# Summing the logits of a sliding-window attention by one reduction, and storing outputs by half tiles

## The chip, the core and the metric

The kernel runs on one core of a Trainium2 chip. The core has TensorE (PE, the matrix multiplier, which reads SBUF and accumulates in PSUM), VectorE (DVE), ScalarE (ACT), GpSimd (POOL) and SyncE (SP, which here only issues DMA transfers). Each engine runs its own instructions in the order in which they were written into the program; semaphores make it wait for others. SBUF is the working memory of 128 partitions, PSUM holds the accumulators in eight banks, of which a 128x512 f32 tile fills one. The metric is the device time of one execution in microseconds (us).

## What is computed

Four layers in a row on a 2048x1024 activation: attention (A), a gated unit (B), A, B, each behind a layer norm and with a residual added. The attention has 32 heads of 32 features and looks at 8 positions, two apart, at or before the query's own:

```
qkv = (x @ wqkv).reshape(B, S, 3, H, Dh)           # H = 32, Dh = 32
idx = pos[:, None] - arange(8)[None, :] * 2        # masked where idx < 0
logits = einsum("bhsd,bhswd->bhsw", q, kg) * Dh**-0.5
attn = softmax(where(mask, logits, -1e9))
o = einsum("bhsw,bhswd->bhsd", attn, vg);  return o.reshape(B, S, D) @ wo
# B: gate = x @ W_gate; up = x @ W_up; (relu(gate) * up) @ W_down, with F = 3584
```

So one logit is a sum over the 32 features of q times a k that lies w*2 positions back. The change is about this sum, and about how the last layer's result goes to memory.

## The kernel before, in words

The 2048 rows are cut into four blocks of 512 (`NB` = 4), each of four tiles of 128 rows (`TPB` = 4). PE does, for each block, the q, k and v projections (`plan_proj`, L364), the output projection (`plan_wo`, L642), gate and up (`plan_gu`, L672) and down (`plan_down`, L718). Every one of these is eight-matmul (or, in down, longer) accumulations into a PSUM tile from one pool of eight (tag `acc`), which is handed round in order. Weights come as slabs of 1 MB through a ring of five buffers (`RING`), loaded by SP (L196) as soon as PE has finished with the slab that had the buffer.

The attention core is not on PE, but on DVE, in "head-major" form: q, k and v go to DRAM and come back with (row tile, head) on the partitions and (feature, position) along the free dimension (L498). For each w of 0 to 7, DVE multiplies q with the shifted k into `pr`, 32 features x 128 positions in bf16, feature outermost (`mul`, L512). Then it sums over the features: `add3` (L522) adds blocks of 8 features three times into an f32 tile `l` of 8x128, and `fold` (L529, L530) halves `l` three times, the last add writing row w of the logits `L`. After eight w comes the softmax in two parts (`soft_a`, L537 to L542, then an exponential on ACT, L545, then `soft_b`, L550 to L555) and eight groups of a times v (`pv_mul`, L563, `pv_add`, L571 to L573), whose results POOL sends to DRAM (L574) and SP fetches back as `oT` (L582) for the output projection. Block 0 of the first layer gets its logits in another way (`first_logits`, on PE); the other seven blocks, three of the first attention layer and four of the second, go through `mul`, `add3` and `fold`: 56 times in all.

DVE also empties PSUM: it multiplies up with the ReLU of gate into `hT` (L687; ACT makes the ReLU `r`, L679, with three buffers), and adds the output projection (L649) and down (L726) to the residual x. ACT copies q, k and v out of PSUM (L373) and does the layer-norm passes (L219, L220, L244).

The order of everything is planned by hand. `Plan` lets each step be booked at a time; PE's order follows from the count of matmuls alone. DVE's attention work is a chain of items `(ready, duration, function, after)`, walked in order by `_place_dve`; the emptying of PSUM and the layer-norm scalars are "fixed" items with due times, and are put in between two chain items as soon as their due time has come. A chain item is not interrupted. The durations in the plan are written out: 2.25 us for `mul`, 1.27 for each of the three adds, 1.5 for `fold`. All other queues (ACT's exponential, SP's loads of q, k, v, POOL's stores) get their place from the times that this walk gives. On the chip nothing is re-ordered.

In the last layer `plan_down` stores the result. For each half (512 columns) of down, and each of the four row tiles, `add` puts the sum into x; for blocks 0 to 2, the store of the full 128x1024 tile (L732, SP) is issued after the second half; for the last block each half is stored by itself (L730, SP or ACT).

Of the kernel before, what the change touches and what calls it, by code (L numbers as in the profile page):

```python
# [10 lines left out]
F32 = mybir.dt.float32  # L11
ALU = mybir.AluOpType
ACT = mybir.ActivationFunctionType

P = 128
D = 1024
H = 32
DH = 32
W = 8
# [4 lines left out]
TPB = BLK // P  # L24
EPS = 1e-5
NEG = -1.0e9
SLAB = 512
# [12 lines left out]
def _ap(t, off, dims):  # L40
    return bass.AP(tensor=t.tensor, offset=t.offset + off, ap=[list(t.ap[0])] + [list(d) for d in dims])
# [78 lines left out]
def kernel(  # L120
# [11 lines left out]
    nc = tc.nc  # L132
# [9 lines left out]
    out_dram = out.flatten_outer_dims()  # L142
# [14 lines left out]
    at_pool = ctx.enter_context(tc.tile_pool(name="attn", bufs=1))  # L157
# [32 lines left out]
    def slab(src_ap, name, start=-10.0):  # L190
        shp = list(src_ap.shape)

        def load():
            t = wring.tile([P, 8, SLAB], BF16, tag="slab", name=name)
            s["t"] = t[:, 0:shp[1], 0:shp[2]]
            nc.sync.dma_start(s["t"], src_ap)  # L196

        s = plan.slab(load, start)
        return s

    plan = Plan(RING)
# [288 lines left out]
    def plan_attn(L, b, ends, st, tm):  # L490
# [16 lines left out]
        def mul(w):  # L507
            def f():
                if w == 0:
                    st["L"] = at_pool.tile([P, W, P], F32, tag="L", name=f"L_{L}_{b}")  # L510
                pr = at_pool.tile([P, DH, P], BF16, tag="pr", name="pr", bufs=2)
                nc.vector.tensor_tensor(pr[:], st["q"][:], _ap(st["k"], HALO - DIL * w, [[HALO + P, DH], [1, P]]),  # L512
                                        op=ALU.mult)
                st["pr"] = pr
            return f

        def add3(i):
            def f():
                if i == 0:
                    st["l"] = at_pool.tile([P, 8, P], F32, tag="l1", name="l1")  # L520
                l, pr = st["l"], st["pr"]
                nc.vector.tensor_tensor(l[:], pr[:, 0:8] if i == 0 else l[:], pr[:, 8 * i + 8:8 * i + 16], op=ALU.add)  # L522
            return f

        def fold(w):
            def f():
                l = st["l"]
                for n in (4, 2):
                    nc.vector.tensor_tensor(l[:, 0:n], l[:, 0:n], l[:, n:2 * n], op=ALU.add)  # L529
                nc.vector.tensor_tensor(st["L"][:, w, :], l[:, 0], l[:, 1], op=ALU.add)  # L530
            return f

        def soft_a():
# [69 lines left out]
        now = lambda: 0.0  # L603
        first = L == 0 and b == 0
        for w in range(0, 0 if first else W):
            plan.chain.append((qk_ready if w == 0 else now, 2.25, mul(w), None))
            for i in range(3):
                plan.chain.append((now, 1.27, add3(i), None))
            plan.chain.append((now, 1.5, fold(w), (lambda t: tm.__setitem__("logits", t)) if w == W - 1 else None))

        def after_a(t):
            plan.at(t + 0.2, expo)
# [88 lines left out]
    def plan_down(L, b, st, last):  # L701
        nsl = (FC + 7) // 8
        accs = {}
        end = last and b == NB - 1

        def cols(half, t):

            n = 2 if end and (half, t) == (1, TPB - 1) else 1
            return [(half * SLAB + i * SLAB // n, SLAB // n) for i in range(n)]

        def mms(half, s8, w, nfc, t):
            def f():
                for c0, n in cols(half, t):
                    if s8 == 0:
                        accs[(t, c0)] = psum.tile([P, n], F32, tag="acc", name="dacc")
                    for jl in range(nfc):
                        j = 8 * s8 + jl
                        nc.tensor.matmul(accs[(t, c0)][:], lhsT=st["hT"][:, j, t * P:(t + 1) * P],  # L718
                                         rhs=w["t"][:, jl, c0 - half * SLAB:c0 - half * SLAB + n],
                                         start=(j == 0), stop=(j == FC - 1))  # L720
            return f

        def add(half, t, c0, n):
            def f():
                xt = x_tiles[b * TPB + t]
                nc.vector.tensor_tensor(xt[:, c0:c0 + n], accs.pop((t, c0))[:], xt[:, c0:c0 + n], op=ALU.add)  # L726
                r0 = (b * TPB + t) * P
                if end:
                    eng = nc.scalar if t == 1 or (t == TPB - 1 and c0 == SLAB) else nc.sync
                    eng.dma_start(out_dram[r0:r0 + P, c0:c0 + n], xt[:, c0:c0 + n])  # L730
                elif last and half == 1:
                    nc.sync.dma_start(out_dram[r0:r0 + P, :], xt[:])  # L732
            return f

        for half in range(2):
            for s8 in range(nsl):
                nfc = min(8, FC - 8 * s8)
                w = slab(wd_v[:, 8 * s8:8 * s8 + nfc, half * SLAB:(half + 1) * SLAB], f"wd_{L}_{b}_{half}_{s8}")
                for t in range(TPB):
                    e = plan.on_pe(nfc, mms(half, s8, w, nfc, t), [w])  # L740
                    if s8 == nsl - 1:
                        pieces = cols(half, t)
                        for i, (c0, n) in enumerate(pieces):
                            plan.on_dve(e + T_EV - 0.4 * (len(pieces) - 1 - i), 0.7, add(half, t, c0, n))
# [9 lines left out]
    def proj(L, b):  # L754
        st, tm = {}, {}
        if L == 0 and b == 0:
            hooks, later_hooks[:] = (lambda h: (h[0], [h[1]]))(first_logits(st, tm))
        else:
            hooks = later_hooks.pop() if later_hooks else {}
        attn[(L, b)] = plan_attn(L, b, plan_proj(L, b, hooks), st, tm)  # L760
# [95 lines left out]
```

## Time and profile before

| | |
|---|---|
| median of 3 runs | 1622.98 us (1622.66 to 1623.08) |
| profiled execution, its own time | 1622.84 us |
| its span in the trace | 1621.1 us |
| PE busy | 1611.6 us (99%) |
| DVE busy | 1014.6 us (63%) |
| ACT busy, POOL busy | 458.1 us, 109.3 us |
| TensorE clock granted | 1.0 throughout |
| DMA moved | 314.83 MB, mean 194 GB/s |
| time of one w on DVE (a `mul`, three adds, a fold), no other work between | 7.49 us (136.30 to 143.79) |

The span runs from the first to the last thing that the profiler saw of the program; the execution's own time has 1.7 us more around it. Busy time of PE is the time in which a matmul is under way. DVE's share of 63% is a mean: until 1255 us, where the last block's attention ends, it is some 90% busy in most stretches, and after that 10 to 20%. Rows of the profile give a line, an engine, the operation, out<-in, the shapes, the count, the busy time, the mean duration of one in ns, and the idle time before them with what ended it.

### The profile page before, as it was taken

How to read it: one execution, taken by the hardware profiler on the slowest of the kernel's cores; microseconds unless marked ns; L12 is line 12 of the kernel's file. 1: busy time of each engine (PE TensorE's matmuls, PEld its weight loads, DVE VectorE, ACT ScalarE, POOL GpSimd, SP SyncE). 2: the span in 40 equal slices, each digit the busy share in tenths (PEclk: the TensorE clock that was granted, in tenths of full speed). 3: DMA queues.
4: the chain of work that ended last, by engine and by line, in shares of the span. 5: the costliest groups of instructions: out<-in, count | busy, mean ns of one | idle time of the engine just before them, and what ended most of it. 6: DMA issues, size and time to landing. Idle time of an engine off the chain costs nothing.

```text
span 1621.1 us, 19223 instructions
## 1 busy us (share of the span) xinstructions
PE 1611.6 (99%) x7641; PEld 740.6 (46%) x7690; DVE 1014.6 (63%) x1256; ACT 458.1 (28%) x735; POOL 109.3 (7%) x174
## 2 busy tenths in 40 slices
PE   9999999999999999999999999999999999999999
PEld 5444444444444444444444444444444444444444
DVE  4576999989989069960699616986989212211211
ACT  6564421304131241312413251133011311221110
POOL 3221000001001100011000110000000000000000
PEclk9999999999999999999999999999999999999999
DMA  8799798597866988669876699599846655565452
GB/s 240 163 199 192 191 218 210 167 217 193 219 173 211 223 206 208 188 200 234 202 198 196 213 223 226 158 279 240 216 154 194 172 182 162 176 173 165 156 167 67
DMA packets 444203, 314.83 MB, mean 194 GB/s; under 512 B 195504, under 2 KB 438608, under 8 KB 444112
## 3 DMA queue, kind: packets, MB, share of 16 engines
q1 hardware_dynamic: 414944, 281.39, 66.7%
q10 hardware_dynamic: 24368, 23.40, 4.7%
q0 software_dynamic: 4800, 8.80, 1.8%
q8 instruction: 60, 0.98, 0.3%
q14 instruction: 31, 0.25, 0.1%
HBM read 261.77 MB, written 36.05 MB: 184 GB/s over the span
## 4 chain that ended last, share of the span: by engine, by line
PE 99%; DMA 0%; DVE 0%; issue 0%; SPq 0%; POOL 0%; DVEq 0%; POOLq 0%
PE acc_g L672 24%; PE acc_u L672 24%; PE dacc L718 24%; PE acc_v L364 7%; PE acc_k L364 7%; PE acc_wo L642 7%; PE acc_q L364 7%; DMA x<-in_A_x_dram 0%; PE L L464 0%; DVE bst L294 0%; POOL rstd L318 0%; DVE xn_all L323 0%; DVE x L726 0%; SPq L785 0%; DVE xnT L331 0%
## 5 line engine op out<-in xcount | busy, mean ns | idle before, releaser
L672 PE MATMUL acc_u<-xnT,wu 128*128 128x512 bf16 x1792 | 423.3, 379 | 0.0
L672 PE MATMUL acc_g<-xnT,wg 128*128 128x512 bf16 x1792 | 423.3, 379 | 0.0
L718 PE MATMUL dacc<-wd,hT 128*128 128x512 bf16 (+1 forms) x1787 | 386.4, 376 | 1.7
L687 DVE TENSOR_TENSOR hT<-acc_u,r 128x512 bf16<-128x512 f32 x224 | 154.1, 688 | 323.9 <-PE acc_u L672 318.3
L679 ACT ACTIVATE r<-acc_g 128x512 bf16<-128x512 f32 x224 | 133.3, 596 | 711.9 <-PE acc_g L672 700.3
L718 PEld LDWEIGHTS <-hT 128*128 128x128 bf16 x1820 | 178.1, 98 | 209.0
L672 PEld LDWEIGHTS <-wu 128*128 128x128 bf16 x1792 | 175.3, 98 | 211.4
L672 PEld LDWEIGHTS <-wg 128*128 128x128 bf16 x1792 | 175.3, 98 | 211.5
L512 DVE TENSOR_TENSOR pr<-qhm,khm 128x4096 bf16<-128x4096 bf16 x56 | 127.9, 2284 | 30.7 <-DMA khm<-k_d 30.6
L563 DVE TENSOR_TENSOR pvt<-a,vhm 128x4096 bf16<-128x4096 bf16 x64 | 146.2, 2285 | 0.2
L522 DVE TENSOR_TENSOR l<-l,pr 128x1024 f32<-128x1024 f32 x112 | 136.8, 1221 | 2.2
L726 DVE TENSOR_TENSOR x<-dacc,x 128x512 bf16<-128x512 f32 (+1 forms) x65 | 43.2, 681 | 126.1 <-PE dacc L718 125.9
L364 PE MATMUL acc_v<-xnT,wv 128*128 128x512 bf16 x512 | 112.0, 379 | 0.0
L642 PE MATMUL acc_wo<-wo,oT 128*128 128x512 bf16 x496 | 111.0, 379 | 0.8
L364 PE MATMUL acc_k<-xnT,wk 128*128 128x512 bf16 x384 | 84.8, 379 | 0.0
L219 ACT ACTIVATE xn_all<-x 128x1024 bf16<-128x1024 bf16 x60 | 63.3, 1055 | 73.8 <-DVE x L649 71.0
L571 DVE TENSOR_TENSOR pvt<-pvt 128x2048 bf16<-128x2048 bf16 x64 | 78.1, 1221 | 1.3
L373 ACT CAST stage_q<-acc_q 128x512 bf16<-128x512 f32 x56 | 32.0, 582 | 162.1 <-PE acc_q L364 153.3
L642 PEld LDWEIGHTS <-oT 128*128 128x128 bf16 x512 | 50.1, 98 | 60.4
L364 PEld LDWEIGHTS <-wv 128*128 128x128 bf16 x512 | 50.1, 98 | 60.2
L244 ACT ACTIVATE xn_all<-x,nb,rstd 128x1024 bf16<-128x1024 bf16 x60 | 71.9, 1233 | 14.2 <-DVE nb L238 11.2
L574 POOL DMA_DIRECT2D o_d<-ohm x64 | 35.2, 550 | 599.7 <-DVE ohm L573 581.7
(76 smaller groups left out, 883.1 us busy)
## 6 DMA issues: line engine op xcount, KB each, us to landing
wg<-in_B_W_gate_dram SPq DMA_DIRECT2D x56, 1024.0 KB, 7.2
wu<-in_B_W_up_dram SPq DMA_DIRECT2D x56, 1024.0 KB, 5.4
wd<-in_B_W_down_dram SPq DMA_DIRECT2D x48, 1024.0 KB, 6.4
wo<-in_A_wo_dram SPq DMA_DIRECT2D x16, 1024.0 KB, 6.9
wv<-in_A_wqkv_dram SPq DMA_DIRECT2D x10, 1024.0 KB, 5.7
wk<-in_A_wqkv_dram SPq DMA_DIRECT2D x9, 1024.0 KB, 5.0
vhm<-v_d SPq DMA_DIRECT2D x32, 284.0 KB, 7.0
v_d<-stage_v ACTq DMA_DIRECT2D x32, 256.0 KB, 6.8
```

The costliest lines, as they stand in the source:

```text
L219: nc.scalar.activation(junk, xt[:], ACT.Identity, accum_out=st[:, 0, t % 2:t % 2 + 1])
L244: nc.scalar.activation(hold["xn"][:, t, :], x_tiles[b * TPB + t][:], ACT.Identity, scale=rstd[:, i:i + 1], bias=nb[:, i:i + 1])
L364: nc.tensor.matmul(acc[:, t0 * P:t1 * P], lhsT=w["t"][:, kc, j * P:(j + 1) * P], rhs=xnT[(L, b)][:, t0:t1, kc, :], start=(kc == 0), stop=( ...
L512: nc.vector.tensor_tensor(pr[:], st["q"][:], _ap(st["k"], HALO - DIL * w, [[HALO + P, DH], [1, P]]), op=ALU.mult)
L522: nc.vector.tensor_tensor(l[:], pr[:, 0:8] if i == 0 else l[:], pr[:, 8 * i + 8:8 * i + 16], op=ALU.add)
L563: nc.vector.tensor_tensor(tt[:], a_bc, v_sh, op=ALU.mult)
L571: nc.vector.tensor_tensor(tt[:, 0:4], tt[:, 0:4], tt[:, 4:8], op=ALU.add)
L642: nc.tensor.matmul(acc[:], lhsT=st["oT"][:, c, t, :], rhs=ws[half]["t"][:, c, :], start=(c == 0), stop=(c == KC - 1))
L672: nc.tensor.matmul(acc[:], lhsT=w["t"][:, kc, (j % 4) * P:(j % 4 + 1) * P], rhs=xnT[(L, b)][:, :, kc, :], start=(kc == 0), stop=(kc == KC ...
L679: nc.scalar.activation(r[:], hold.pop(("g", j))[:], ACT.Relu)
L687: nc.vector.tensor_tensor(st["hT"][:, j, :], hold.pop(("u", j))[:], hold.pop(("r", j))[:], op=ALU.mult)
L718: nc.tensor.matmul(accs[(t, c0)][:], lhsT=st["hT"][:, j, t * P:(t + 1) * P], rhs=w["t"][:, jl, c0 - half * SLAB:c0 - half * SLAB + n], sta ...
```

## The change

The six adds per w become one reduction instruction, which reads `pr` with the feature as the innermost index (the access pattern `[[1, P], [P, DH]]`: 128 positions one element apart, and for each of them 32 features, 128 elements, 256 bytes, apart) and writes 128 sums to `L`. The tile `l` is gone. In the plan the four chain items of a w after `mul` become one of 4.4 us. In the last layer, blocks 0 to 2 store each half tile right after its add, on SP; the last block does what it did.

```diff
-        def add3(i):
-            def f():
-                if i == 0:
-                    st["l"] = at_pool.tile([P, 8, P], F32, tag="l1", name="l1")
-                l, pr = st["l"], st["pr"]
-                nc.vector.tensor_tensor(l[:], pr[:, 0:8] if i == 0 else l[:], pr[:, 8 * i + 8:8 * i + 16], op=ALU.add)
-            return f
-
         def fold(w):
             def f():
-                l = st["l"]
-                for n in (4, 2):
-                    nc.vector.tensor_tensor(l[:, 0:n], l[:, 0:n], l[:, n:2 * n], op=ALU.add)
-                nc.vector.tensor_tensor(st["L"][:, w, :], l[:, 0], l[:, 1], op=ALU.add)
+                nc.vector.tensor_reduce(st["L"][:, w, :], _ap(st["pr"], 0, [[1, P], [P, DH]]),
+                                        axis=mybir.AxisListType.X, op=ALU.add)
             return f
...
             plan.chain.append((qk_ready if w == 0 else now, 2.25, mul(w), None))
-            for i in range(3):
-                plan.chain.append((now, 1.27, add3(i), None))
-            plan.chain.append((now, 1.5, fold(w), (lambda t: tm.__setitem__("logits", t)) if w == W - 1 else None))
+            plan.chain.append((now, 4.4, fold(w), (lambda t: tm.__setitem__("logits", t)) if w == W - 1 else None))
...
                 r0 = (b * TPB + t) * P
-                if end:
-                    eng = nc.scalar if t == 1 or (t == TPB - 1 and c0 == SLAB) else nc.sync
+                if last:
+                    eng = nc.scalar if end and (t == 1 or (t == TPB - 1 and c0 == SLAB)) else nc.sync
                     eng.dma_start(out_dram[r0:r0 + P, c0:c0 + n], xt[:, c0:c0 + n])
-                elif last and half == 1:
-                    nc.sync.dma_start(out_dram[r0:r0 + P, :], xt[:])
             return f
```

In the changed program PE's instructions stand in the same order as before. On DVE, ACT, POOL and SP the order changes, since the plan books each w 0.91 us shorter (7.56 us before, 6.65 after), 7.3 us per block.

## The prediction

> **What bounds the kernel now.** I read the page from its busy shares to its chain of waits, then what PE waited for, then DVE's groups with shapes kept apart, then DVE's timeline around the first block that the change touches.
>
> ```profile
> PE 1611.6 (99%) x7641; PEld 740.6 (46%) x7690; DVE 1014.6 (63%) x1256; ACT 458.1 (28%) x735; POOL 109.3 (7%) x174
> ...
> DVE  4576999989989069960699616986989212211211
> ...
> PE 99%; DMA 0%; DVE 0%; issue 0%; SPq 0%; POOL 0%; DVEq 0%; POOLq 0%
> ```
>
> The chain that ended last is matmuls, 99% of the span. DVE's digits say the other half: in slices 4 to 31 it is near full, with a few holes, so its mean of 63% says nothing about the stretches in which logits are made.
>
> ```profile
> PE warm L289 <- POOL neg_half L177: 1.4, 1, 1.4
> PE acc_q L364 <- DMA wqk<-in_A_wqkv_dram: 0.7, 1, 0.7
> PE tp L328 <- DVE xn_all L323: 0.7, 1, 0.7
> PE acc_q L364 <- ACT xnT L331: 0.5, 2, 0.2
> ```
>
> This is all that PE waited for (total us, times, longest): 3.3 us, all on tiles of the start-up of block 0, which the change does not touch. After that PE never waits, neither for DVE nor for a slab. So there is next to nothing to gain, and the question is whether DVE, ACT or SP can now hold PE up.
>
> **The sum over the features.** What is removed, and the rows nearest to what comes in:
>
> ```profile
> L522 DVE TENSOR_TENSOR l<-l,pr 128x1024 f32<-128x1024 f32 x112 | 136.8, 1221 | 2.2
> L522 DVE TENSOR_TENSOR l<-pr 128x1024 f32<-128x1024 bf16 x56 | 68.3, 1219 | 0.6
> L529 DVE TENSOR_TENSOR l<-l 128x512 f32<-128x512 f32 x56 | 38.5, 687 | 1.0
> L529 DVE TENSOR_TENSOR l<-l 128x256 f32<-128x256 f32 x56 | 23.8, 425 | 1.9
> L530 DVE TENSOR_TENSOR L<-l 128x128 f32<-128x128 f32 x56 | 16.4, 292 | 1.9
> L512 DVE TENSOR_TENSOR pr<-qhm,khm 128x4096 bf16<-128x4096 bf16 x56 | 127.9, 2284 | 30.7 <-DMA khm<-k_d 30.6
> L294 DVE BATCH_NORM_STATS2 bst<-x 128x6 f32<-128x512 bf16 x6 | 3.9, 686 | 3.6 <-DMA x<-in_A_x_dram 3.6
> L537 DVE TENSOR_TENSOR L<-L,maskc 32x112 f32<-32x112 f32 x2 | 0.5, 264 | 3.6 <-ACT L L473 3.6
> ```
>
> Removed: 136.8 + 68.3 + 38.5 + 23.8 + 16.4 = 283.8 us of DVE, 5.07 us per w. Added: 56 reductions of 4096 bf16 to 128 f32. No row shows one, nor any DVE read in which each element lies 256 bytes from the last, so I bound it. Low: 2.28 us, the product of 4096 elements (L512), which is no slower than two elements at a time. Middle: one element at a time. From 512 to 1024 f32 elements the adds grow by 1221 - 687 = 534 ns, 1.043 ns each; the statistics of L294, a true one-input reduction, need 686 ns for 512 bf16, the same. So 687 + 3584 x 1.043 = 4425 ns. High: if each of the 32 blocks of 128 cost what a separate add of 128 does (L530), 32 x 292 = 9.34 us. I take 4.42: L294 is the nearest kind, and the mask's add of L537, whose 112 elements lie in eight runs of 14 in `L`, takes 264 ns where the line through 292 (128) and 687 (512) gives 275, so eight jumps cost nothing. That they cost nothing is shown for one jump in 14 elements, not for one at every element. Then 56 x 4.42 = 247.5 us; DVE's busy time falls by 36 to about 978 us, and one w from 7.49 to 2.32 (start of a product to start of what follows) + 4.42 = 6.74, 0.75 less, 6.0 us per block. All of it lies under PE's matmuls: worth 0 us.
>
> [...]
>
> **What DVE's order does to PE.** DVE also empties PSUM, in its written order, so a chain item that is longer than planned pushes back every `hT` behind it. The tightest place is the first block with logits by this route, when gate and up of block 0 begin at 194.97 us:
>
> ```profile
> 194.97 1.73 PE acc_g L672 x8
> ...
> 204.33 1.23 DVE L542 TENSOR_TENSOR L<-L,m 128x1024 f32<-128x1024 f32 x1
> 205.47 0.68 DVE L687 TENSOR_TENSOR hT<-acc_u,r 128x512 bf16<-128x512 f32 x1
> 206.68 0.69 DVE L550 TENSOR_TENSOR ssum<-L 128x512 f32<-128x512 f32 x1 [0.52 <-ACT L L545]
> ...
> 210.32 1.28 DVE L687 TENSOR_TENSOR hT<-acc_u,r 128x512 bf16<-128x512 f32 x2
> ```
>
> A PSUM tile takes PE 1.727 us (6.91 for four) and eight go round, so up tile 0 (the second) must be empty when the tenth begins, at 194.97 + 9 x 1.727 = 210.5, and up tile 1 at 214.0. Before, they are empty at 206.15 and 211.0: spare 4.4 and 3.0. After, the softmax's first part ends at 205.56 - 6.0 = 199.6; the exponential (1.1) and the second part (206.68 to 210.40, 3.7) end at 204.5. The new order puts one `pv_mul` (2.3) ahead of the first `hT`, which ends at 207.4, and a `pv_add` (2.3) ahead of the next, 210.4: spare 3.1 and 3.6. So PE still doesn't wait, with the same least reserve as now: it begins to wait when a reduction takes 4.42 + 3.1 / 8 = 4.8 us. A single item of 4.42 in place of pieces of at most 2.28 holds an `hT`, or an add of L649 or L726, up to 2.2 us longer; in the later blocks the timeline shows DVE idle for PE between its `hT` (0.2 to 0.9 us), so nearly the whole round of 7 x 1.727 = 12.1 us is reserve.
>
> **ACT, POOL and SP.** In the first of these blocks the exponential now stands ahead of the last two copies of v. ACT waits at it from about 192 to 199.6 (before it waited 8.26 us, for the same end of L542, two copies later), so the tiles of v, done at 193.2 and 195.0, are empty at 201.9; PE wants them 12.1 us after they are done, from 205.3 on. Cost 0, cover 3.4 us. POOL's `rstd` moves behind stores of `ohm` in places; the layer norms concerned have a down stage of 48 us (305 to 353) or more before their use. SP's loads of q and k still wait for the last product that reads the old ones; that comes earlier too. The stores:
>
> ```profile
> out_dram<-x SPq DMA_DIRECT2D x12, 256.0 KB, 4.6
> out_dram<-x SPq DMA_DIRECT2D x5, 128.0 KB, 1.7
> ...
> SPq L732 <- DVE x L726: 8.1, 9, 3.4
> ```
>
> Twelve stores of 256 KB become 24 of 128 KB, with the same bytes. An issue of the half-tile kind takes SP 0.33 us (L730), so 12 x 0.33 = 4 us more over three blocks, in a queue that spends 445 us waiting for PE to finish gate tiles. The four new ones per block each wait for an add behind at most a reduction; before, the stores' longest wait was 3.4 us, now I expect up to 3.4 + 2.2. Behind them stand slabs: the wu load issued at 207.09 is first used at 194.97 + 27.6 + 1.7 = 224.3 and lands in 5.4, so 11.8 us of delay are free. Cost 0. The tail stays: the last block's stores are as before.
>
> Sum: 1622.84 (its span 1621.1 and 1.7 around it) - 0 + 0 = 1622.8; the profiled execution lies 0.14 under the median of 1622.98, so I say 1623.0.
>
> **Rivals.** *A, slower: the reduction pays for each jump.* It decides above 4.8 us. At the high end of 9.34 one w takes 11.66, 4.17 more than now, 33.4 per block. The first block loses 8 x (9.34 - 4.42) - 3.1 = 36.3. The next two follow without a rest, so the lag is never paid back: 33.4 less what DVE idles now in their stretches (256.2 to 388.5: 8.8; 390.2 to 524.5: 11.5), 24.6 and 21.9. The last four begin with DVE waiting for PE, so they have 12.1 more: with idle 11.0, 11.2, 7.3, 7.7, they lose 10.3, 10.1, 14.0, 13.6. Together 131: 1754 us. For it: no row shows such a read. Against: L294 and L537. *B, a queue becomes the bound:* SP stands at a half-tile store for two whole w, 13.5 us, beyond the 11.8 free, or an `hT` falls behind by more than 3.1; some 2 us in two or three places, 1627. For it: the reserves are small. Against: no PE wait on a slab or on DVE anywhere now. *C, faster:* the freed 36 us remove a wait of PE. All 3.3 us are at the start, and even their whole would give 1619.7; against it is that no DVE work of the change lies there.
>
> **How the numbers follow.** No change by more than 0.2% (3.2 us, about what can be told from no change): 0.54. A: 0.37, because the one price that matters has no row; its time lies anywhere from 1627 to 1754, the middle of it at 1690. B: 0.07, of which half stays within 0.2%. C: 0.02. So faster 0.02, same 0.57, slower 0.41. The likeliest case alone gives 1621.5 to 1625; to leave out no more than two in ten the range takes in B and the larger part of A: 1621 to 1740.
>
> **What would show it.** Right: reductions of 4.3 to 4.5 us, DVE busy near 978 us, PE's waits as above and no line with `hT` or a slab. Wrong by A: reductions over 4.8 us, PE waits of `acc_g` and `acc_u` on DVE `hT`, most after the first block, and DVE's slices full. Wrong by B: PE waits on a `wd`, `wg` or `wu` load, or SP waiting over 11.8 us at the new stores.

## The result and the profile after

The changed kernel takes 1722.13 us (median of 6 runs, 1721.42 to 1723.72) against 1622.96 (6 runs) before: ratio 1.0613, 95% interval 1.0599 to 1.0626. It is 99 us slower. The profiled execution has a span of 1720.7 us, 99.6 more than before.

The page of the changed kernel: busy times and shares, DVE and granted PE clock in 40 slices, the shares of the chain that ended last by engine and by line, and the new operation's row.

```profile
PE 1641.4 (95%) x7690; PEld 745.9 (43%) x7690; DVE 1128.3 (66%) x976; ACT 455.2 (26%) x735; POOL 111.1 (6%) x174
...
DVE  4668999999998049990599805997899512121111
...
PEclk9999999999999999999999999999989999999999
...
PE 67%; DVE 27%; issue 4%; DMA 1%; SPq 0%; POOL 0%; ACT 0%; DVEq 0%; POOLq 0%; ACTq 0%
PE dacc L706 18%; DVE L L519 17%; PE acc_g L660 15%; PE acc_u L660 15%; PE acc_k L364 5%; PE acc_v L364 5%; DVE pr L512 5%; PE acc_q L364 5%; PE acc_wo L630 3%; DVE hT L675 2%; DVE pvt L553 1%; DVE x L637 1%; DVE x L714 0%; DVE pvt L561 0%; SPq L250 0%
...
L519 DVE TENSOR_REDUCE L<-pr 128x128 f32<-128x4096 bf16 x56 | 399.3, 7131 | 0.6
```

A reduction takes 7.13 us, not 4.42. DVE has 114 us more to do than before instead of 36 less, and the chain that ended last, which was 99% PE, now runs over DVE for 27% of the span, 17% of it in the reductions. DVE is still busy for only 66% of the span: it is no bound by its sum.

What PE waited for in the changed kernel (total us, times, longest), without the waits of the start:

```profile
PE acc_u L660 <- DVE hT L675: 19.1, 8, 4.0
PE acc_g L660 <- DVE hT L675: 14.0, 9, 3.5
PE acc_wo L630 <- DVE hT L675: 10.6, 6, 2.2
PE acc_u L660 <- DVE x L714: 8.7, 1, 8.7
PE acc_q L364 <- DVE x L637: 8.1, 3, 4.6
PE acc_g L660 <- ACT stage_v L373: 6.4, 1, 6.4
```

With four smaller ones (2.2, 1.7, 1.6, 0.2) these are 72.6 us. All are waits for a PSUM tile that DVE has not emptied yet, or (the last row) that ACT has not, because it stands at the exponential and waits there for DVE (18.0 us, until 221.55). The rest is clock. The stretches around that 6.4 us wait (us, then busy time and count of each engine; the last three columns are granted PE clock, DMA share, GB/s):

```profile
215.00:223.00 8.00, 1.70 (x8) 0.69 (x7) 6.74 (x6) 1.45 (x3) 0.00 (x0) 0.83 1.09 217
223.00:227.00 4.00, 3.87 (x10) 1.36 (x10) 3.83 (x6) 2.14 (x5) 0.00 (x0) 0.50 0.19 66
227.00:235.00 8.00, 8.00 (x38) 3.60 (x37) 7.93 (x9) 1.19 (x2) 0.59 (x1) 0.99 0.98 244
```

After the wait PE has half its clock for 4 us, and does 10 matmuls in them where it would do 18. Over the whole span the granted clock is 0.984; 0.016 x 1720.7 = 27.5 us. Waits and clock make 100.1 for a difference of 99.6; the two overlap a little, since the clock falls while PE still waits (0.83 from 219 to 221 us and 0.50 from 221 to 223, where PE does no matmul). PE's busy time says nearly the same: 1641.4 us here, 1615.0 in run 3 below, whose trace has as many matmuls at full clock, so 26.4 us are slower matmuls.

Where the waits come from is seen on DVE's timeline (start, us, operation) between two reductions in the first block of the second attention layer:

```profile
647.84 0.69 DVE L675 TENSOR_TENSOR hT<-acc_u,r 128x512 bf16<-128x512 f32 x1
648.45 7.16 DVE L519 TENSOR_REDUCE L<-pr 128x128 f32<-128x4096 bf16 x1
655.53 0.14 DVE L238 SCALAR_TENSOR_TENSOR nb<-mean,rstd 128x2 f32<-128x2 f32 x1
655.60 1.27 DVE L675 TENSOR_TENSOR hT<-acc_u,r 128x512 bf16<-128x512 f32 x2
656.80 2.27 DVE L512 TENSOR_TENSOR pr<-qhm,khm 128x4096 bf16<-128x4096 bf16 x1
659.00 0.67 DVE L675 TENSOR_TENSOR hT<-acc_u,r 128x512 bf16<-128x512 f32 x1
659.60 7.13 DVE L519 TENSOR_REDUCE L<-pr 128x128 f32<-128x4096 bf16 x1
```

From one reduction to the next DVE needs 11.15 us and does three `hT`; other w have only two. PE makes one in 3.45 us, 3.2 in that time. The order was written for a reduction of 4.4 us, so it has too few `hT` per w, and DVE falls behind PE.

### The profile page after: what moved, and what is told of

The parts are those of the page before. It is cut to its first block, busy times and chain, and to the rows that moved or that the text cites. A ratio compares the mean times of both kernels' runs of the same rounds, so it can differ in the third digit from the quotient of the medians.

```text
span 1720.7 us, 19017 instructions
## 1 busy us (share of the span) xinstructions
PE 1641.4 (95%) x7690; PEld 745.9 (43%) x7690; DVE 1128.3 (66%) x976; ACT 455.2 (26%) x735; POOL 111.1 (6%) x174
## 4 chain that ended last, share of the span: by engine, by line
PE 67%; DVE 27%; issue 4%; DMA 1%; SPq 0%; POOL 0%; ACT 0%; DVEq 0%; POOLq 0%; ACTq 0%
PE dacc L706 18%; DVE L L519 17%; PE acc_g L660 15%; PE acc_u L660 15%; PE acc_k L364 5%; PE acc_v L364 5%; DVE pr L512 5%; PE acc_q L364 5%; PE acc_wo L630 3%; DVE hT L675 2%; DVE pvt L553 1%; DVE x L637 1%; DVE x L714 0%; DVE pvt L561 0%; SPq L250 0%
## 5 line engine op out<-in xcount | busy, mean ns | idle before, releaser
L660 PE MATMUL acc_u<-xnT,wu 128*128 128x512 bf16 x1792 | 431.5, 384 | 27.8 <-DVE hT L675 19.1
L660 PE MATMUL acc_g<-xnT,wg 128*128 128x512 bf16 x1792 | 429.3, 383 | 22.0 <-DVE hT L675 14.0
L519 DVE TENSOR_REDUCE L<-pr 128x128 f32<-128x4096 bf16 x56 | 399.3, 7131 | 0.6
L630 PE MATMUL acc_wo<-wo,oT 128*128 128x512 bf16 x512 | 115.0, 384 | 10.6 <-DVE hT L675 10.6
L561 DVE TENSOR_TENSOR pvt<-pvt 128x2048 bf16<-128x2048 bf16 x64 | 78.1, 1221 | 1.4
L233 POOL TENSOR_TENSOR rstd<-vpe,neg_half 128x2 f32<-128x2 f32 x30 | 33.3, 1109 | 611.2 <-DVE vpe L231 610.5
```

Source lines behind the costliest of these rows:

```text
L519: nc.vector.tensor_reduce(st["L"][:, w, :], _ap(st["pr"], 0, [[1, P], [P, DH]]), axis=mybir.AxisListType.X, op=ALU.add)
L561: nc.vector.tensor_tensor(tt[:, 0:4], tt[:, 0:4], tt[:, 4:8], op=ALU.add)
L630: nc.tensor.matmul(acc[:], lhsT=st["oT"][:, c, t, :], rhs=ws[half]["t"][:, c, :], start=(c == 0), stop=(c == KC - 1))
L660: nc.tensor.matmul(acc[:], lhsT=w["t"][:, kc, (j % 4) * P:(j % 4 + 1) * P], rhs=xnT[(L, b)][:, :, kc, :], start=(kc == 0), stop=(kc == KC ...
```

## The experiments

**1 and 2: the two parts of the change alone.** The first run has the new stores and the six adds, the second the reduction and the old stores:

```diff
# 1, on the kernel before
-                if end:
+                if last:
...
# 2, on the changed kernel
-                if last:
+                if end:
...
+                elif last and half == 1:
+                    nc.sync.dma_start(out_dram[r0:r0 + P, :], xt[:])
```

> Only the half-tile stores of the change; the six adds stay. My theory (the loss is all the reduction's): the time of before, 1623.0 us within 0.5, PE's waits the 3.3 us of the start. Rival (the stores, waiting for adds ahead of slab loads in SP's queue, hold PE up): 3 us or more over before, with PE waits on a weight slab in the last layer. If the stores carry a part of the loss of 99, this kernel shows it alone.

> Only the reduction and its plan; full-tile stores as before. My theory: the whole loss, 1722 us within 2 us, reductions at 7.13 us. Rival (a part of the loss is the stores'): below 1719 us.

Stores alone: 1622.86 us (11 runs), ratio 1.0000 (0.9991 to 1.0008). Reduction alone: 1722.61 us, ratio 1.0611 (1.0597 to 1.0626). The stores cost and bring nothing; the loss is the reduction's.

**3: the same reduction, read in order.**

```diff
-                nc.vector.tensor_reduce(st["L"][:, w, :], _ap(st["pr"], 0, [[1, P], [P, DH]]),
+                nc.vector.tensor_reduce(st["L"][:, w, :], _ap(st["pr"], 0, [[DH, P], [1, DH]]),
```

> The changed kernel with one edit: the reduction reads the same 4096 elements of the product tile in the order in which they lie, 32 neighbours per sum, so it adds other products than the reference's logits. Plan, orders, stores and counts are those of the changed kernel. My theory (the 256-byte step between the elements is what costs): the reduction takes 4.4 us, as the prediction had it, PE waits only 3.3 us at the start, 1623.0 us within 1. Rival 1 (a reduction of bf16 to f32 is slow in itself): 7.1 us and 1722 us. Rival 2 (the new order on DVE, ACT and SP costs PE time even at 4.4 us): the reduction takes 4.4 us but the time is 1627 us or more.

The row of the reduction in this run, and all that PE waited for in it:

```profile
L519 DVE TENSOR_REDUCE L<-pr 128x128 f32<-128x4096 bf16 x56 | 247.0, 4411 | 0.6
```

```profile
PE warm L289 <- POOL neg_half L177: 1.4, 1, 1.4
PE acc_q L364 <- DMA wqk<-in_A_wqkv_dram: 0.7, 1, 0.7
PE acc_q L364 <- ACT xnT L331: 0.5, 2, 0.2
```

1622.70 us, ratio 0.9999 (0.9990 to 1.0008). Same operation, elements, plan and orders: the step between the elements is all that differs, and with it comes the whole loss. My 4.42 us was right for this reduction, to 0.01 us.

**4: which steps cost.** Inside `fold`, a step of s elements for each w, over the same 4096; and the softmax's maximum as one reduction:

```diff
+                def go(s):
+                    out = _ap(st["L"], w * P, [[s, P // s], [1, s]])
+                    return out, _ap(st["pr"], 0, [[DH * s, P // s], [1, s], [s, DH]])
...
-            nc.vector.tensor_tensor(m[:], Lt[:, 0:4], Lt[:, 4:8], op=ALU.max)
...
+            nc.vector.tensor_reduce(m[:, 0], _ap(Lt, 0, [[1, P], [P, W]]), axis=mybir.AxisListType.X, op=ALU.max)
```

> The changed kernel with another step between the 32 elements of a sum for each w (1, 4, 8, 16, 2, 32, 64, 128 elements of 2 bytes for w = 0 to 7, so the sums are other ones than the reference's), and the softmax's maximum as one reduction over w of 1024 f32 with a step of 512 bytes in place of three maxima. Only the durations matter here. [...] Rival (the cost grows with the step): a ramp between 16 and 256 bytes. Rival (the cost is one of bf16 reads, not of jumps): the f32 maximum takes 1.22 us.

The whole kernel took 1676.66 us (one run); only DVE's groups by shape are used here. The lines stand for steps of 2 bytes (L524), 4 (L532), 8 (L526), 16 (L528), 32 (L530), 64 (L534), 128 (L536), 256 (L538); L547 is the maximum, f32, 512 bytes:

```profile
L530 DVE TENSOR_REDUCE L<-pr 128x128 f32<-128x4096 bf16 x7 | 52.8, 7547 | 0.1
L528 DVE TENSOR_REDUCE L<-pr 128x128 f32<-128x4096 bf16 x7 | 52.3, 7466 | 0.0
L536 DVE TENSOR_REDUCE L<-pr 128x128 f32<-128x4096 bf16 x7 | 50.3, 7180 | 0.0
L538 DVE TENSOR_REDUCE L<-pr 128x128 f32<-128x4096 bf16 x7 | 49.8, 7120 | 0.1
L534 DVE TENSOR_REDUCE L<-pr 128x128 f32<-128x4096 bf16 x7 | 49.2, 7027 | 0.0
L526 DVE TENSOR_REDUCE L<-pr 128x128 f32<-128x4096 bf16 x7 | 30.9, 4415 | 0.1
L532 DVE TENSOR_REDUCE L<-pr 128x128 f32<-128x4096 bf16 x7 | 30.9, 4414 | 0.1
L524 DVE TENSOR_REDUCE L<-pr 128x128 f32<-128x4096 bf16 x7 | 30.9, 4411 | 0.1
L547 DVE TENSOR_REDUCE m<-L 128x128 f32<-128x1024 f32 x8 | 15.2, 1900 | 0.1
```

There are two levels and nothing between: 4.41 us up to 8 bytes, 7.0 to 7.5 from 16 bytes on. The upper level costs 0.64 to 0.77 ns more for each element; why 16 and 32 bytes cost a little more than 64 to 256 is not shown. The f32 maximum, at 512 bytes, pays about the same: 1.90 us, where 1024 elements read in order would take about 1.22, an estimate from the row of the adds (1221 ns), since no run has this maximum in order; the difference is 0.66 ns for each element. At 256 bytes the price is 2.71 us for 4096 elements (7.12 against 4.41), also 0.66 ns each, some two thirds of the 1.04 ns by which the adds grow with each element.

**5: the plan told the truth.**

```diff
-            plan.chain.append((now, 4.4, fold(w), (lambda t: tm.__setitem__("logits", t)) if w == W - 1 else None))
+            plan.chain.append((now, 7.15, fold(w), (lambda t: tm.__setitem__("logits", t)) if w == W - 1 else None))
```

> The changed kernel with one number edited: the plan books the reduction at 7.15 us, what it takes, in place of 4.4, so the items that empty PSUM stand in DVE's order where PE needs them. Instructions and their durations stay. Theory 1 (PE loses because DVE's written order is too short by 8 x 2.7 = 22 us per block, and DVE's own idle time lies behind the logits where it can't help): PE's waits on hT nearly vanish; what is left is the late oT of the first two blocks, which the plan itself now books 5.7 and 1.5 us after PE wants it, and some clock loss: 1630 to 1645 us. Theory 2 (DVE simply has 115 us too much to do in the stretches with logits, whatever the order): 1700 us or more. The sum on record for the slower rival, put at 7.13 us, counts all of DVE's idle time as usable and gives 30 us, 1653; that would fit neither.

1624.95 us (10 runs), ratio 1.0015 (1.0006 to 1.0024). 97 of the 99 us come back by one number in the plan, with the slow instruction still there: its page has DVE at 1132.9 us, PE at 1611.7. It is better than I expected of either theory; the late `oT` that the plan books cost nothing that the trace shows. On its DVE timeline, the same stretch of work as above:

```profile
601.70 7.18 DVE L519 TENSOR_REDUCE L<-pr 128x128 f32<-128x4096 bf16 x1
608.80 1.28 DVE L675 TENSOR_TENSOR hT<-acc_u,r 128x512 bf16<-128x512 f32 x2
611.46 0.69 DVE L675 TENSOR_TENSOR hT<-acc_u,r 128x512 bf16<-128x512 f32 x1 [1.37 <-PE acc_u L660]
612.06 2.28 DVE L512 TENSOR_TENSOR pr<-qhm,khm 128x4096 bf16<-128x4096 bf16 x1
614.91 0.69 DVE L675 TENSOR_TENSOR hT<-acc_u,r 128x512 bf16<-128x512 f32 x1 [0.56 <-PE acc_u L660]
615.52 7.15 DVE L519 TENSOR_REDUCE L<-pr 128x128 f32<-128x4096 bf16 x1
```

Four `hT` between two reductions, and DVE even waits for PE (in brackets). The one wait of PE that is new in this run is for an add of the first output projection (L637) that stands behind a reduction:

```profile
PE acc_q L364 <- DVE x L637: 1.8, 1, 1.8
```

**6 and 7: how much lag PE takes.** One or three slow w in eight, the others read in order:

```diff
-                nc.vector.tensor_reduce(st["L"][:, w, :], _ap(st["pr"], 0, [[1, P], [P, DH]]),
-                                        axis=mybir.AxisListType.X, op=ALU.add)
+                step = [[1, P], [P, DH]] if w < 1 else [[DH, P], [1, DH]]      # 7: w < 3
+                nc.vector.tensor_reduce(st["L"][:, w, :], _ap(st["pr"], 0, step), axis=mybir.AxisListType.X, op=ALU.add)
```

> The changed kernel, in which only w = 0 of a block reads with the 256-byte step and the other seven read 32 neighbours, so these seven sum other products than the reference's. One slow reduction puts DVE 2.7 us behind its plan per block. The recorded reserve of 3.1 us: no wait of PE, 1623.0 us within 1. Rival (any lag costs PE): 3 us or more, 1626 up.

> As the run with one slow w, but with three slow w of eight (w = 0 to 2), the other five read neighbours and sum other products. DVE falls 8.1 us behind its plan per block. Recorded reserve: the first block with logits passes its 3.1 to 4.6 us and costs PE 3.5 to 5 us, the later ones stay inside 12.1 us: 1627 to 1632 us with some clock loss. Rival 1 (loss in proportion to the slow reductions): 99 x 3/8 = 37 us, 1660 us. Rival 2 (all reserves are larger than I thought): 1623 us.

One of eight: 1625.13 us (11 runs), ratio 1.0013 (1.0005 to 1.0022), 2 us where I expected none. Three of eight: 1639.83 us, ratio 1.0103 (1.0088 to 1.0119), between my expectation and the proportion. Both fail at the same place, as PE's waits say (the first row is of the run with one slow w, the other two of the run with three):

```profile
PE acc_q L364 <- DVE x L637: 2.1, 2, 1.9
...
PE acc_q L364 <- DVE x L637: 7.3, 3, 4.6
PE acc_u L660 <- DVE x L714: 3.5, 1, 3.5
```

The first two rows are in the first block with logits, at 155 to 166 us: the adds of the output projection wait behind a reduction, and the projection after it waits for their PSUM tiles. That is some 45 us ahead of the `hT` that I had taken for the tightest. Four of these adds begin at 160.29 us in run 6, 12.65 after its second reduction (147.64). In run 3 that reduction begins at 144.33, so the same work would put the adds at 156.98, an estimate. They are 3.3 later in run 6, and PE waits 2.1: the reserve here is some 1.2 us, not 3.1. The third row is the same kind of place at the end of a down stage. In the run with three, waits for `hT` are 0.3 us, and with its waits of 11.1, the clock of 0.997 (4.9 us) fills the difference.

**8: the product written in the order in which it is to be read.**

```diff
-                nc.vector.tensor_tensor(pr[:], st["q"][:], _ap(st["k"], HALO - DIL * w, [[HALO + P, DH], [1, P]]),
+                nc.vector.tensor_tensor(_ap(pr, 0, [[1, DH], [DH, P]]), st["q"][:], _ap(st["k"], HALO - DIL * w, [[HALO + P, DH], [1, P]]),
...
-                nc.vector.tensor_reduce(st["L"][:, w, :], _ap(st["pr"], 0, [[1, P], [P, DH]]),
+                nc.vector.tensor_reduce(st["L"][:, w, :], _ap(st["pr"], 0, [[DH, P], [1, DH]]),
...
-            plan.chain.append((qk_ready if w == 0 else now, 2.25, mul(w), None))
+            plan.chain.append((qk_ready if w == 0 else now, 4.4, mul(w), None))
```

> The product is written with the feature innermost (each written element 64 bytes from the last), the reduction reads 32 neighbours, the plan books 4.4 us for each. If only reads pay for steps: product 4.4 us (one element at a time, no longer two), reduction 4.41, one w 8.8 us, and with a true plan PE loses little: 1623 to 1640 us. If writes pay too: product 7 us or more, DVE falls behind its plan by 21 us per block, and the time is near that of the changed kernel, 1700 us or more.

2325.51 us, ratio 1.4331 (1.4311 to 1.4351), far beyond both. The product's and the reduction's rows of this run:

```profile
L512 DVE TENSOR_TENSOR pr<-qhm,khm 128x4096 bf16<-128x4096 bf16 x56 | 1011.6, 18065 | 19.5 <-DMA v_d<-stage_v 14.5 <-DMA khm<-k_d 5.0
L519 DVE TENSOR_REDUCE L<-pr 128x128 f32<-128x4096 bf16 x56 | 247.3, 4417 | 0.3
```

The reduction gets its 4.42 us, and the product written with a step of 64 bytes takes 18.07 us, 15.8 more than the dense one (2.28).

**9: the lag without the slow instruction.** Read in order, 4.41 us each, but booked too short by what the changed kernel's are:

```diff
-                nc.vector.tensor_reduce(st["L"][:, w, :], _ap(st["pr"], 0, [[1, P], [P, DH]]),
+                nc.vector.tensor_reduce(st["L"][:, w, :], _ap(st["pr"], 0, [[DH, P], [1, DH]]),
...
-            plan.chain.append((now, 4.4, fold(w), (lambda t: tm.__setitem__("logits", t)) if w == W - 1 else None))
+            plan.chain.append((now, 1.7, fold(w), (lambda t: tm.__setitem__("logits", t)) if w == W - 1 else None))
```

> The contiguous reduction (32 neighbours per sum, so other products are added than the reference's), which takes 4.41 us, but booked in the plan at 1.7 us, so that DVE falls 8 x 2.71 = 21.7 us behind its plan in each block, as much as in the changed kernel, with DVE as little loaded as before. Theory 1 (the loss is the difference between what the plan books and what the chip takes, whatever the instruction): 1690 to 1740 us, with the same kinds of PE wait. Theory 2 (it needs the slow instruction and the DVE time it takes): within 8 us of 1623.

1717.14 us, ratio 1.0581 (1.0563 to 1.0599). DVE has less to do than before the change (980.1 us), and PE waits at the same kinds of place:

```profile
PE acc_u L660 <- DVE hT L675: 22.7, 13, 3.6
PE acc_u L660 <- DVE x L714: 22.1, 2, 14.8
PE acc_g L660 <- DVE hT L675: 17.0, 5, 5.5
```

With run 5 this closes it: the slow instruction with a true plan costs 2 us, a fast one with a plan as wrong costs 94. What PE loses comes from the difference between what the plan books and what the chip takes, and not from the time that the instruction adds to DVE.

**10: writes with a step.** The product with a step of s elements for each of w = 0 to 4, by the same kind of pattern as in run 4, read in order.

```diff
+                    return (_ap(pr, 0, [[P * s, DH // s], [1, s], [s, P]]), _ap(st["q"], 0, [[P * s, DH // s], [P, s], [1, P]]),
+                            _ap(st["k"], HALO - DIL * w, [[(HALO + P) * s, DH // s], [HALO + P, s], [1, P]]))
```

> The product written with a step of 2, 4, 8, 16 and 32 elements of 2 bytes for w = 0 to 4, and dense for the rest; the reduction reads 32 neighbours, so the sums are other ones than the reference's for all w but w = 4. Only the product's durations matter. Dense 2.28 us and 64 bytes 18.07 us are known. [...] Rival (every bf16 element written alone costs the same, since it is less than a word): 18 us already at 4 bytes.

The whole kernel took 1960.98 us (one run). DVE's groups: L526 is dense, L516 4 bytes, L518 8, L520 16, L522 32, L524 64:

```profile
L520 DVE TENSOR_TENSOR pr<-qhm,khm 128x4096 bf16<-128x4096 bf16 x7 | 128.4, 18336 | 0.0
L524 DVE TENSOR_TENSOR pr<-qhm,khm 128x4096 bf16<-128x4096 bf16 x7 | 126.1, 18015 | 0.0
L522 DVE TENSOR_TENSOR pr<-qhm,khm 128x4096 bf16<-128x4096 bf16 x7 | 121.5, 17360 | 0.0
L518 DVE TENSOR_TENSOR pr<-qhm,khm 128x4096 bf16<-128x4096 bf16 x7 | 65.2, 9314 | 0.0
L526 DVE TENSOR_TENSOR pr<-qhm,khm 128x4096 bf16<-128x4096 bf16 x21 | 48.1, 2289 | 0.0
L516 DVE TENSOR_TENSOR pr<-qhm,khm 128x4096 bf16<-128x4096 bf16 x7 | 33.4, 4770 | 33.0 <-DMA khm<-k_d 33.0
```

The recorded 18 us at 4 bytes did not come: it is 4.77 us at 4 bytes, 9.31 at 8, then 17.4 to 18.3 from 16 to 64. The time about doubles at each step up to 16 bytes and then stays there. Divided by the number of 16-byte stretches that the writes go to one after the other, the measured time comes, as an estimate, to 4.7 ns (1024 stretches at a step of 4 bytes), 4.5 (2048 at 8 bytes) and 4.2 to 4.5 (4096 from 16 bytes on), and the dense product, with 512, to 4.5 as well; whether the same thing bounds the dense product was not tried. Why a write with such a step costs about 4.4 ns (18 us over 4096) and a read only 0.7 more than an element is not shown.

## Why the prediction was right in its rival and wrong in its forecast

The forecast was 1623.0 us, no change (0.57); what came is A, the slower rival (0.37). Two steps of the forecast failed, the duration of the reduction and the price of the lag that it makes.

- *What bounds the kernel, and that nothing is to be gained:* held. Reading in order, with 33 us less DVE work than before, brings 0.3 us of 1623, within the interval.
- *Stores, SP, POOL:* held; the stores alone give a ratio of 1.0000.
- *The duration of the reduction: this step failed.* "I take 4.42: L294 is the nearest kind, and the mask's add of L537 ... eight jumps cost nothing." L294 reads 512 neighbours, L537 runs of 14 f32, 56 bytes: in both, most elements lie next to the one read before. No row stood for a jump at every element, as the prediction itself said, and from that gap the value came out as the cheap end. The chip took 7.13 us; of the steps tried in run 4, those of up to 8 bytes took 4.41 and those from 16 on 7.0 to 7.5.
- *DVE's order as the way in which it hurts:* held in kind, and where "A" was to be seen it is: waits of `acc_g` and `acc_u` on `hT`, and ACT's copies of v behind the exponential, whose cover of 3.4 us I had named, as the largest wait of that block.
- *The point from which it decides, 4.8 us:* worked out for the wrong place. I had taken the first `hT` for the tightest, with 3.1 us; the adds of the output projection ahead of it have some 1.2, so that in run 6, with a mean of 4.76 us, PE already waits 2.1 us. The 4.8 itself is not tested by that: in run 6 all of the extra 2.7 us come with w = 0, while eight equal reductions of 4.76 us would have put DVE only some 1 us behind at that place, where three of the eight have run.
- *The price of A: the second step that failed.* The sum took "33.4 less what DVE idles now in their stretches". At the measured 7.13 the same sum gives 18.6 (8 x 2.71 - 3.1) for the first block, then 8 x 1.96 = 15.7 less 8.8 and 11.5, and nothing for the last four: 30 us, 1653. The chip lost 99. DVE's idle time can't be used where it is needed, because the order is written for the booked durations (in run 5, whose order is written for 7.15, the same added work costs PE only 2 us): the lag is 8 x 2.73 = 21.8 us per block against the plan, not 15.7 less idle against the kernel before. Runs 5 and 9 show it from both sides. The measured 1722 lies inside the stated range only because its slow end stood on a reduction of 9.34 us, more than the chip takes, in a sum that gives too little (30 us at 7.13): two errors that ran against each other, which is luck. The clock, some 26 us, was not in the sum at all.

No version here beats the kernel before: with a true plan PE is as busy as before (1611.7 us against 1611.6), and less work on DVE alone, as in run 3, wins nothing.

## What to carry to other kernels

Before a reduction is turned across a tile, look at the step of its innermost index in bytes: if no row of the profile reads with such a step, the cost is open, and the neighbour that reads in order is no witness. In a kernel whose queues are ordered by booked durations, a duration that is booked too short costs by itself, and can cost far more than the slow instruction (here 94 us in run 9 against 2 in run 5); after a change measure the new instruction and put its time back into the plan before judging the change. And idle time of an engine counts as reserve only where its written order lets it be used.

## What was not expected of the hardware

- Reductions on DVE that read with a step of 16 to 256 bytes took 7.0 to 7.5 us in place of 4.41 for 4096 bf16, 0.64 to 0.77 ns more for each element, in a single jump between 8 and 16 bytes; the maximum of 1024 f32 with a step of 512 bytes took 1.90 us, against an estimate of 1.22 in order.
- DVE writes of single bf16 elements with a step are far dearer: 4.77, 9.31 and 17.4 to 18.3 us for 4 bytes, 8 bytes, and 16 to 64, against 2.29 dense.
- After some waits PE is slow for a while: the granted clock was 0.50 for 4 us after the wait of 6.4, and after one of 2.2 (at 909.6 us) eight matmuls took 3.45 us at a granted clock of 0.52, where their row is 1.89 at full clock; after others of 2.2 (at 303.4 and 699.4 us) it was 1.89. What decides was not tried.
